# Sliding-window attention followed by a two-layer network on one core: most of the second layer by one level of Strassen's method

## The chip, the cores and the metric

The kernel runs on one core of one Trainium2 chip. The metric is device time in microseconds (us), from the start of the program to its end on that core; a time quoted here is the median of several executions unless it says otherwise. Lower is better. The five engines of the core appear as PE (TensorE, matrix products), DVE (VectorE), ACT (ScalarE), POOL (GpSimd) and SP (SyncE, which issues transfers). PEld is the loading of weights into PE, which runs beside its products.

## The reference

Attention over 4 batches of 768 tokens, 8 heads of 64, where a token sees the first 4 tokens and the last 128; then, on all 3072 tokens, a dense layer, a squared relu and a second dense layer.

```python
scores = scale * np.matmul(q, k.transpose(0, 1, 3, 2))
keep = is_sink | in_window                       # n_sink = 4, window = 128
scores = np.where(keep, scores, -1000000000.0)
a = np.exp(scores - np.max(scores, axis=-1, keepdims=True))
a = a / (np.sum(a, axis=-1, keepdims=True) + 1e-09)
attn_out = np.matmul(a, v)                       # (4, 8, 768, 64)
x = attn_out.transpose(0, 2, 1, 3).reshape(3072, 512)
r = np.maximum(x @ w_in, 0.0)                    # w_in 512 x 2048
return ((r * r) @ w_out).astype(np.float32)      # w_out 2048 x 512
```

The kernel holds its operands in bf16 and accumulates in fp32.

## The kernel before

The program doesn't write its instructions in the order of its text. It first lists operations, each with the engines that could do it, estimated durations, the operations that it must follow and the buffers that it takes. A planner then simulates the engines and emits the operations one by one in the order, and on the engine, that comes out earliest; `key` breaks ties between operations that could start at the same time.

```python
LATENCY = 0.2
PE_SLACK = 0.334
...
                for e, c in o.engines.items():
                    slack = PE_SLACK if e == "pe" else 0.0
                    start = max([t + slack if t > 0 else 0.0, engine.get(e, 0.0)] +
                                [a.end + LATENCY + slack for a in o.after if a.engine != e or a.dma] +
                                [a.issued for a in o.follow])
                    if pick is None or start + c < pick[1] + pick[2]:
                        pick = (e, start, c)
                cand = (round(pick[1], 2), o.key)
```

Attention computes the scores of a block of 256 tokens, takes exp on ACT, masks the result on DVE or POOL, multiplies with v, normalises into `xn_sb` and turns that into `xT` (by PE and a copy, or for batches 2 and 3 by a transposing DMA):

```python
                            if e == "dve":
                                mk = (mask if s else mask0).rearrange("p h a c -> p h (a c)")
                                nc.vector.tensor_mul(x[:, :, o:512], x[:, :, o:512], mk[:, :, o:512])
                            ...
                            else:
                                y = x.rearrange("p h (i g c) -> p g (h i) c", i=2, g=2)
                                for i in range(2):
                                    triangles(y[:, i], i, 4)         # an affine select on POOL
```

The two dense layers. `pm` and `py` are PSUM tiles of two banks each, and both come from one pool of two:

```python
    def layer1(b, key, fbs, c0, cw, need):
        ...
            for i, fb in enumerate(fbs):
                for kb in range(NKB):
                    nc.tensor.matmul(pm[:, i, :], lhsT=w_in_sb[:, fb // 4, kb, fb % 4:512:4],
                                     rhs=xT[:, c0 // 256:(c0 + cw) // 256, kb, :], start=(kb == 0), stop=(kb == NKB - 1))
        ...
                nc.scalar.activation(out=r, in_=bank_t.pop(tag), func=AF.Relu)
        ...
            (nc.vector if e == "dve" else nc.gpsimd).tensor_mul(
                gT_sb[c0 // 512][:, fbs[0]:fbs[0] + n, c0 % 512:c0 % 512 + cw], r, r)

    def layer2(b, u, keys, by_part=False):
        ...
                for fb in range(4 * part, 4 * part + 4):
                    nc.tensor.matmul(pm[:, i, :], lhsT=gT_sb[t // 4][:, fb, 128 * (t % 4):128 * (t % 4) + 128],
                                     rhs=w_out_sb[:, fb, :], start=(fb == 0), stop=(fb == NFB - 1))
```

Layer 2 takes a pair of token tiles (2 x 128 tokens) at a time: 32 products of 512 columns, then one copy out of PSUM and one store. There are 12 pairs, three a batch.

The softmax here doesn't subtract the row's maximum and nothing guards it: scores larger than these inputs give would overflow.

Of the kernel before, what the change touches and what calls it, by code (L numbers as in the profile page):

```python
# [16 lines left out]
LATENCY = 0.2  # L17
PE_SLACK = 0.334
DMA_START = {"sp": 1.2, "act": 1.2, "pool": 1.6}
DMA_LATENCY = 0.9  # L20
WARM_UNTIL = 34.0

# [10 lines left out]
class Op:  # L33
    def __init__(self, key, engines, run, after, takes, reads, dma, follow):
        self.key, self.engines, self.run = key, engines, run
        self.after, self.takes, self.reads, self.dma = list(after), list(takes), list(reads), dma
        self.follow, self.yields, self.margin = list(follow), [], 0.0
        self.end = self.issued = self.engine = None


class Plan:
# [8 lines left out]
    def __init__(self, capacity):  # L50
        self.ops, self.capacity = [], dict(capacity)

    def op(self, key, engines, run, after=(), takes=(), reads=(), dma=0.0, follow=()):
        o = Op(key, engines, run, after, takes, reads, dma, follow)
        self.ops.append(o)
        return o

    def run(self):
# [12 lines left out]
        while left:  # L71
            best = None
            for o in ready:
# [7 lines left out]
                for p, n in need.items():  # L81
                    if len(free[p]) < n:
                        ok = False
                        break
                    t = max(t, sorted(free[p])[n - 1] + LATENCY)
# [48 lines left out]
def kernel(  # L134
# [23 lines left out]
    NSINK = 4  # L158
# [4 lines left out]
    sizes = dict(att=2, den=2, qr=5, qs=6, expm=8, r=3, osb=2)  # L163
# [9 lines left out]
    mask = consts.tile([128, 2, 4, 128], BF16)  # L173
    mask0 = consts.tile([128, 2, 4, 128], BF16)
    bias = consts.tile([128, 4, 128], BF16)
    bias0 = consts.tile([128, 4, 128], BF16)
# [10 lines left out]
    xT_sb = [consts.tile([128, NS, NKB, 256], BF16, name=f"xT{i}") for i in range(2)]  # L187
    gT_sb = [consts.tile([128, NFB, w], BF16, name=f"gT{i}") for i, w in enumerate((512, 256))]
# [15 lines left out]
    def copy(e, dst, src):  # L204
        if e == "act":
            nc.scalar.activation(out=dst, in_=src, func=AF.Copy)  # L206
        elif e == "dve":
            nc.vector.tensor_copy(out=dst, in_=src)  # L208
        else:
            nc.gpsimd.tensor_copy(out=dst, in_=src)  # L210
# [41 lines left out]
    def build_masks(e):  # L252
        for h2 in range(2):
            for i in range(2):
                nc.gpsimd.tensor_copy(out=mask[:, h2, 2 * i:2 * i + 2, :], in_=tri)
                nc.gpsimd.tensor_copy(out=mask0[:, h2, 2 * i:2 * i + 2, :], in_=tri)
            nc.gpsimd.memset(mask0[0:NSINK, h2, 1:3, :], 1.0)
# [10 lines left out]
    c_fill = op(-9, {"dve": 2.5}, fill)  # L268
# [26 lines left out]

    def load_w_in(i, behind=None, yields=()):
# [24 lines left out]
    ROW = {256: 0.0205, 512: 0.028, 1024: 0.046, 1536: 0.068}  # L321
# [80 lines left out]
    def attention(b, key):  # L402
# [16 lines left out]
        def stage(g, f0, f1, side):  # L419

# [24 lines left out]
            for m in range(0, NP, w) if b not in NATURAL else ():  # L445
# [21 lines left out]
                def transpose(e, m=m, bs=bs):  # L467
                    pt = bank_t[b, m, g] = bank(bs, "pt", [128, 2, 1024], BF16)
                    warm(pt[:, 0, 0:128])
                    qs = {ti: qs_t.pop((b, m, ti, g)) for ti in (1, 0)}  # L470
                    for j in range(w):
                        for ti in (1, 0):
                            for t in range(n):

                                o = 128 * n * ti if w == 2 else 0
                                nc.tensor.matmul(  # L476
                                    pt[:, j if w == 2 else ti, o + 128 * t:o + 128 * t + 128],
                                    lhsT=qs[ti][:, j, t, :, :], rhs=ident, is_transpose=True,
                                    start=(t == 0 and (w == 1 or ti == 1)), stop=(t == n - 1 and (w == 1 or ti == 0)))
                tr = op(at(f + 0.03), {"pe": 0.02 + 0.11 * n * w}, transpose,  # L480
                        after=regs + [c_ident] + prev_scores + prev_sinks,
                        takes=[bs], reads=[qs_slot[b, m, ti, g] for ti in (0, 1)])
                ops["transpose", b, m, g] = tr
                for j in range(2):
                    def unload(e, m=m, j=j):

                        if w == 2:
                            copy(e,
                                 qkT_sb[:, m + j, :, t0 // 128:last // 128, :].rearrange(
                                     "c i a b -> c i (a b)").rearrange("c i (p t) -> c i p t", t=n),  # L490
                                 bank_t[b, m, g][:, j, 0:256 * n].rearrange("c (i t p) -> c i p t", i=2, t=n))
                        else:
                            copy(e,
                                 qkT_sb[:, m, j, t0 // 128:last // 128, :].rearrange(
                                     "c a b -> c (a b)").rearrange("c (p t) -> c p t", t=n),
                                 bank_t[b, m, g][:, j, 0:128 * n].rearrange("c (t p) -> c p t", t=n))
                    c = op(at(f + 0.04), {"dve": 0.1 + w * n * 0.14, "act": 0.19 + w * n * 0.107}, unload,
                           after=[tr] + prev_scores + prev_sinks, reads=[bs])
# [5 lines left out]
            if g == 0:  # L504
# [7 lines left out]
                def sink_values(e):  # L512
                    for j in range(NP):
# [9 lines left out]
                                    after=([ops["turn", b, 1, 0]] if b in NATURAL else copies) + prev_sinks)  # L523
            lo = max(256, t0)
# [20 lines left out]
            for s in range(t0 // 256, last // 256):  # L545
                fs = 0.36 + 0.5 * (256 * s - t0) / (last - t0)
                norms = []
                biased = b == 0 and s < BIASED
                for m0 in (0, 2):
# [27 lines left out]
                    for ms in ((m0,), (m0 + 1,)) if b == 0 else ((m0, m0 + 1),):  # L577
                        sc.append(op(
                            at(fm), {"pe": len(ms) * (0.7 if biased else 0.28) + 0.1}, lambda e, f=scores, ms=ms: f(e, ms),
                            takes=[banks[m - m0] for m in ms],  # L580
                            after=[ops["turn", b, ti, t] for ti in (0, 1)
# [5 lines left out]
                    for j, m in enumerate((m0, m0 + 1)):  # L587
# [7 lines left out]
                        def domask(e, s=s, m=m, o=o):  # L595
                            x = ex_t[b, s, m]
                            if e == "dve":
                                mk = (mask if s else mask0).rearrange("p h a c -> p h (a c)")
                                nc.vector.tensor_mul(x[:, :, o:512], x[:, :, o:512], mk[:, :, o:512])  # L599
                            elif s == 0:  # L600
                                mk = mask0.rearrange("p h a c -> p h (a c)")
                                nc.gpsimd.tensor_mul(x[:, :, o:512], x[:, :, o:512], mk[:, :, o:512])
# [4 lines left out]
                        if biased:  # L607
# [4 lines left out]
                                         {"pool": 1.3, "dve": 0.7} if s else {"dve": 0.58, "pool": 1.1},  # L612
                                         domask, after=[ex] if first else [ex, late["masks"]]))

                    bo = Slot(side, 1)

                    def values(e, s=s, m0=m0, bo=bo):
                        po = bank_t["o", b, s, m0] = bank(bo, "po", [128, 2, 512], FP32)
                        warm(po[:, 0, 0:128])
                        for j, m in enumerate((m0, m0 + 1)):  # L620
                            x = ex_t.pop((b, s, m))
                            pv = po[:, j, 0:4 * (D + 1)].rearrange("p (i h d) -> p i h d", i=2, d=D + 1)
                            mms = []
                            for h2 in range(2):
                                h = 2 * m + h2
                                for i in range(2):
                                    t = 2 * s + i
                                    if t >= 1:
# [247 lines left out]
```

## Time and profile before

| | before |
|---|---|
| median of 3 runs | 226.12 us (225.82 to 226.16) |
| span of the profiled run | 223.8 us |
| first product of layer 1 | 20.76 us |
| last product of layer 2 ends | 219.87 us |
| PE, DVE, ACT, POOL busy | 215.5, 103.7, 115.9, 64.8 us |

Two more lines of the kernel before are needed later. The first is one row of the table of stretches, from 53 to 78 us; its columns are the stretch, its length, the busy time of PE, PEld, DVE, ACT and POOL with the number of instructions, the clock, the share of the DMA engines and GB/s:

```profile
53.00:78.00 25.00, 24.41 (x274) 18.30 (x277) 16.58 (x31) 16.70 (x23) 21.38 (x25) 1.00 1.89 156
```

PE is idle for 25.00 - 24.41 = 0.59 us in it, and DVE is busy for two thirds. The second is from the groups of instructions by form, the masking on POOL:

```profile
L222 POOL TENSOR_SCALAR_AFFINE_SELECT expm<-expm 128x512 bf16<-128x512 bf16 x2 | 1.2, 634 | 6.5 <-ACT expm L590 6.5
```

Only two such selects are done here after the start, 634 ns each. The other masks are products on DVE.

### The profile page before, as it was taken

How to read it: one execution, taken by the hardware profiler on the slowest of the kernel's cores; microseconds unless marked ns; L12 is line 12 of the kernel's file. 1: busy time of each engine (PE TensorE's matmuls, PEld its weight loads, DVE VectorE, ACT ScalarE, POOL GpSimd, SP SyncE). 2: the span in 40 equal slices, each digit the busy share in tenths (PEclk: the TensorE clock that was granted, in tenths of full speed). 3: DMA queues.
4: the chain of work that ended last, by engine and by line, in shares of the span. 5: the costliest groups of instructions: out<-in, count | busy, mean ns of one | idle time of the engine just before them, and what ended most of it. 6: DMA issues, size and time to landing. Idle time of an engine off the chain costs nothing.

```text
span 223.8 us, 4586 instructions
## 1 busy us (share of the span) xinstructions
PE 215.5 (96%) x1932; PEld 138.2 (62%) x1952; DVE 103.7 (46%) x192; ACT 115.9 (52%) x131; POOL 64.8 (29%) x99
## 2 busy tenths in 40 slices
PE   7899999999999999999999999999999999999993
PEld 7549996467865886555454545598464455874441
DVE  6646346476656764466452536657241024430010
ACT  2695566506893577286727188665351165551010
POOL 7991015055999415997100000000000000000000
PEclk9999999999999999999999999999999999999999
DMA  5999968998999999999999464020221320000222
GB/s 144 289 187 208 208 196 109 199 349 240 131 179 139 150 197 150 122 150 199 143 144 124 139 166 48 0 50 0 47 98 25 116 97 0 0 3 0 94 103 86
DMA packets 84309, 28.13 MB, mean 126 GB/s; under 512 B 70336, under 2 KB 80832, under 8 KB 84288
## 3 DMA queue, kind: packets, MB, share of 16 engines
q0 software_dynamic: 52608, 10.49, 61.9%
q1 hardware_dynamic: 31496, 17.20, 34.9%
q8 instruction: 15, 0.25, 0.4%
q10 hardware_dynamic: 184, 0.14, 0.2%
q14 instruction: 6, 0.05, 0.1%
HBM read 27.30 MB, written 6.29 MB: 150 GB/s over the span
## 4 chain that ended last, share of the span: by engine, by line
PE 91%; DMA 3%; SPq 2%; ACT 1%; DVE 1%; issue 1%; DVEq 0%
PE pm L694 38%; PE py L734 37%; PE po L634 6%; PE ps L571 5%; DMA qr<-in_q_dram 3%; PE pt L476 2%; SPq L348 2%; PE px L671 1%; DVE qkT L208 1%; PE ps L564 1%; PE pk L531 0%; ACT r L703 0%; ACT expm L590 0%; ACT qkT L206 0%; PE px L201 0%
## 5 line engine op out<-in xcount | busy, mean ns | idle before, releaser
L734 PE MATMUL py<-w_out_sb,gT 128*128 128x512 bf16 x366 | 86.1, 379 | 1.1 <-issue 0.3
L694 PE MATMUL pm<-xT,w_in_sb 128*128 128x256 bf16 (+1 forms) x576 | 86.7, 308 | 0.4 <-ACT r L703 0.3
L694 PEld LDWEIGHTS <-w_in_sb 128*128 128x128 bf16 x576 | 63.0, 114 | 20.9 <-issue 1.7
L703 ACT ACTIVATE r<-pm 128x1024 bf16<-128x1024 f32 x48 | 49.2, 1025 | 32.7 <-PE pm L694 23.9
L734 PEld LDWEIGHTS <-gT 128*128 128x128 bf16 x384 | 35.4, 98 | 39.2 <-issue 1.7
L710 DVE TENSOR_TENSOR gT<-r 128x1024 bf16<-128x1024 bf16 x48 | 33.1, 690 | 50.3 <-ACT r L703 50.2
L590 ACT ACTIVATE expm<-ps 128x1024 bf16<-128x1024 f32 (+1 forms) x48 | 43.2, 952 | 17.1 <-PE ps L571 17.1
L599 DVE TENSOR_TENSOR expm<-expm,mask 128x1024 bf16<-128x1024 bf16 (+1 forms) x39 | 25.4, 654 | 23.7 <-ACT expm L590 23.2
L206 ACT ACTIVATE osb<-py 128x1024 f32<-128x1024 f32 x9 | 9.2, 1024 | 31.2 <-PE py L734 31.1
L634 PEld LDWEIGHTS <-expm 128*128 128x128 bf16 x352 | 16.5, 97 | 4.1 <-issue 0.6
L634 PE MATMUL po<-v,expm 128*128 128x65 bf16 x352 | 17.5, 193 | 0.0
L646 DVE TENSOR_TENSOR xn_sb<-po,rc 128x512 bf16<-128x512 f32 x24 | 16.6, 691 | 0.8
L571 PE MATMUL ps<-qkT 64*128 64x128 bf16 (+1 forms) x256 | 14.8, 238 | 0.3
L571 PEld LDWEIGHTS <-qkT 64*128 64x128 bf16 x256 | 8.0, 94 | 10.7 <-issue 9.9
L634 PE MATMUL po<-vs,es 128*128 128x65 bf16 x128 | 13.1, 193 | 0.0
L208 DVE COPY osb<-py 128x1024 f32<-128x1024 f32 (+2 forms) x4 | 3.6, 889 | 19.0 <-PE py L734 15.9
L210 POOL CAST qs<-qr 128x512 bf16<-128x512 f32 x6 | 4.2, 714 | 26.2 <-DVE gT L710 14.1
L634 PEld LDWEIGHTS <-es 128*128 128x128 bf16 x128 | 11.7, 97 | 0.0
L390 POOL DMA_DIRECT2D v<-in_v_dram x12 | 10.8, 918 | 3.4 <-DMA qn<-in_q_dram 2.5
L380 POOL DMA_DIRECT2D qn<-in_q_dram x12 | 10.8, 918 | 1.5 <-DMA qn<-in_k_dram 1.2
L361 POOL DMA_DIRECT2D v<-in_v_dram x12 | 10.9, 926 | 0.5 <-DMA qr<-in_k_dram 0.5
L208 DVE CAST qs<-qr 128x512 bf16<-128x512 f32 x16 | 8.1, 513 | 6.2 <-DMA qr<-in_k_dram 3.1
(51 smaller groups left out, 108.1 us busy)
## 6 DMA issues: line engine op xcount, KB each, us to landing
out_dram<-osb SPq DMA_DIRECT2D x11, 512.0 KB, 2.8
v<-in_v_dram POOLq DMA_DIRECT2D x24, 128.0 KB, 6.5
qr<-in_k_dram SPq DMA_DIRECT2D x8, 256.0 KB, 5.2
qr<-in_q_dram SPq DMA_DIRECT2D x8, 256.0 KB, 4.9
w_in_sb<-in_moe_w_in_dram POOLq DMA_DIRECT2D x4, 512.0 KB, 9.8
w_out_sb<-in_moe_w_out_dram POOLq DMA_DIRECT2D x4, 512.0 KB, 10.8
qn<-in_k_dram POOLq DMA_DIRECT2D x12, 128.0 KB, 7.2
qn<-in_q_dram POOLq DMA_DIRECT2D x12, 128.0 KB, 8.8
```

What stands on the lines that cost most here:

```text
L208: nc.vector.tensor_copy(out=dst, in_=src)
L361: return [nc.gpsimd.dma_start(out=v_sb[b % 2][:, t, :, 0:D], in_=v[b, :, 128 * t:128 * t + 128, :].rearrange("h p d -> p h d"))]
L380: return [nc.gpsimd.dma_start(out=qn_t[b, ti][:, t, :].rearrange("p (h d) -> p h d", d=D), in_=(q, k)[ti][b, :, 128 * t:128 * t + 128, :]. ...
L571: nc.tensor.matmul(ps[:, h2, o:o + w], lhsT=qkT_sb[r, m, 1, c, :], rhs=qkT_sb[r, m, 0, qb:qb + w // 128, :], start=(i == 0 and not biased) ...
L590: nc.scalar.activation(out=x[:, :, o:512], in_=bank_t["s", b, s, m][:, :, o:512], func=AF.Exp, scale=scale)
L599: nc.vector.tensor_mul(x[:, :, o:512], x[:, :, o:512], mk[:, :, o:512])
L634: nc.tensor.matmul(pv[:, i, h2, :], lhsT=lhsT, rhs=rhs, start=(n_ == 0), stop=(n_ == len(mms) - 1))
L646: nc.vector.tensor_tensor(out=xn_sb[:, 2 * s:2 * s + 2, 128 * m0:128 * m0 + 256].rearrange("p i (j h d) -> p j i h d", j=2, d=D), in0=pv[: ...
L694: nc.tensor.matmul(pm[:, i, :], lhsT=w_in_sb[:, fb // 4, kb, fb % 4:512:4], rhs=xT[:, c0 // 256:(c0 + cw) // 256, kb, :], start=(kb == 0), ...
L703: nc.scalar.activation(out=r, in_=bank_t.pop(tag), func=AF.Relu)
L710: (nc.vector if e == "dve" else nc.gpsimd).tensor_mul(gT_sb[c0 // 512][:, fbs[0]:fbs[0] + n, c0 % 512:c0 % 512 + cw], r, r)
L734: nc.tensor.matmul(pm[:, i, :], lhsT=gT_sb[t // 4][:, fb, 128 * (t % 4):128 * (t % 4) + 128], rhs=w_out_sb[:, fb, :], start=(fb == 0), sto ...
```

## The change

The intent has four parts.

- **Strassen.** For ten of the twelve pairs, the 256 x 2048 by 2048 x 512 product of layer 2 is cut into 2 x 2 blocks and done in seven block products instead of eight. Four sums of blocks of the activations a pair (`s1` to `s4`) and four sums of weight blocks, once, are new work for DVE, and so are the sums of the products.
- **Unordered banks.** A tile of two banks used to be one thing for the scheduler: a read of it waited for every earlier write. `touch` now declares that accesses to different banks of a tile, by PE and another engine, need no order.
- **A finer start.** For the first 512 tokens keys are transposed before queries arrive, values and norms go head pair by head pair, and the turn into `xT` goes in two halves.
- **A table of shifts** (`PLACES`) of the planner's keys, with smaller planned latencies. The masks become smaller constants, so that room is free, and a masking that the planner gives to DVE reads `tri`.

```diff
-LATENCY = 0.2
-PE_SLACK = 0.334
+LATENCY = 0.145
+PE_SLACK = 0.0
+PLACES = {
+    ('att', 0, 0): (-0.11, 0.89), ('att', 0, 1): (0.01, 0.98), ('att', 1, 0): (0.12, 1.07),
 ... (85 groups of operations in all)
+    def touch(t, e, ins, *banks, alone=False):
+        before = touched.setdefault(t, [])
+        for e_, ins_, banks_, alone_ in before:
+            apart = (e == "pe") != (e_ == "pe") or e != e_ and alone and alone_
+            if apart and not set(banks) & set(banks_):
+                tc.declare_no_dep(ins.ins, ins_.ins, reason="other bank")
+        before.append((e, ins, banks, alone))
 ...
 ... transposes: keys, then queries
+                for part in ((1,), (0,)) if w == 1 else ((1, 0),):
 ... values and norms by head pair
+                    parts = ((0,), (1,)) if b == 0 and s < 2 else ((0, 1),)
 ... relu: reads PSUM at a step of two, so that a tile gets the even tokens, the next the odd ones
+            h = bank_t.pop(tag).rearrange("p n (a q e) -> p (n a) e q", q=128, e=2)
+            o = r.rearrange("p n (a e q) -> p (n a) e q", q=128, e=2)
 ...
+        for n, x, y in ((1, b12, b11), (3, b22, b12), (2, b22, 1), (4, b21, 2)):
 ...
+                nc.vector.tensor_tensor(out=wt_sb[n], in0=x, in1=y, op=ALU.subtract)
 ... layer2_fast, for all pairs but the first two of batch 0
+        o1 = total("s1", a21, a22, ALU.add, s1_, key(0), low + high, [])
+        o3 = total("s3", a11, a21, ALU.subtract, None, key(0), low + [o1], [])
+        o2 = total("s2", "s1", a11, ALU.subtract, s2_, key(0), [o1], [s1_])
+        o4 = total("s4", a12, "s2", ALU.subtract, s4_, key(0), [o2], [s2_])
 ...
+        p5 = product(0, "c", "s1", 1, True, [o1, ops["wt", 1]], [bs], [s1_])
+        p7 = product(1, "d", "s3", 3, True, [o3, ops["wt", 3]])
+        x0 = taken("x", "c", os_, 0, [p5])
+        p1 = product(2, "a", a11, w(0, 0), False, low, [ys] if tail else [])
+        p6 = product(3, "b", "s2", 2, False, [o2, ops["wt", 2], x0], (), [s2_])
+        u0 = taken("u", "a", us, 2, [p1])
+        ex = pair_sum("x", "d", 2, [x0, p7 if tail else p1])
+        p3 = product(4, "c", "s4", w(1, 1), False, [x0, o4], (), [s4_])
+        p4 = product(5, "d", a22, 4, False, [ex, ops["wt", 4]] + ([] if tail else [u0]))
+        eu = pair_sum("u", "b", 4, [u0, p3])
 ...
+        p2 = product(6, "a", a12, w(1, 0), False, [u0] + high)
```

Each `product` is eight matmuls of 256 columns. `c` and `b` lie in the first bank of the pair's tile and `d` and `a` in the second, and `taken` and `pair_sum` read one bank while the next product fills the other.

## The prediction

> **What bounds the kernel now.** First the page's head: busy time of each engine.
>
> ```profile
> PE 215.5 (96%) x1932; PEld 138.2 (62%) x1952; DVE 103.7 (46%) x192; ACT 115.9 (52%) x131; POOL 64.8 (29%) x99
> ```
>
> TensorE (PE) is busy for 96% of a 223.8 us span (the timed median, 226.12 us, is 2.3 us more; I carry that difference over), VectorE (DVE) and ScalarE (ACT) for about half. A busy PE may still be a waiting PE, so next the chain that ended last, in order of time:
>
> ```profile
> 4.50 5.75 DMA qr<-in_q_dram
> ...
> 10.35 0.50 DVE qs L208
> 10.85 1.80 DVE qkT L208 x3
> ...
> 12.67 0.60 ACT qkT L206
> 13.27 0.92 ACT expm L590
> ...
> 18.03 0.45 PE po L201 x8
> 18.48 0.73 PE po L634 x24
> 19.20 0.45 PE px L671 x8
> 19.65 0.56 PE px L201 x10
> 20.21 0.53 PE px L671 x8
> ...
> 20.76 14.13 PE pm L694 x128
> ...
> 75.80 3.50 PE pm L694 x32
> ...
> 199.40 10.74 PE py L734 x49
> 210.14 0.05 issue
> 210.19 9.67 PE py L734 x44
> 219.87 0.02 issue
> 219.89 0.39 ACT half L206
> 220.28 0.02 issue
> 220.31 0.42 DVE osb L208
> ```
>
> Three stretches. To 20.76 us the chain passes from the last load of q through DVE and ACT to PE: latency of the first 512 tokens. L201 in it are warming matmuls, which compute nothing. From 20.76 to 219.87 us (199.1 us) every piece but about 1.1 us is PE work. After 219.87 us come two evictions, one behind the other although neither reads what the other writes, and the last store. So a matmul removed after 20.76 us should shorten the end by its issue time, if what replaces it on the other engines keeps up.
>
> The price of a matmul comes from the chain, not from the group's mean (379 ns for `py`, which overlaps its neighbours). From 199.13 to 219.87 us PE does three pairs of token tiles, 96 matmuls of 512 columns (94 are recorded): 20.74/96 = 0.216 us. Those of 256 columns cost 3.50/32 = 0.1094 us and 14.13/128 = 0.1104 us. Each has its own weight load, so a load per 256 columns is hidden in this kernel already.
>
> The durations that the new vector work needs are in the groups by form:
>
> ```profile
> L710 DVE TENSOR_TENSOR gT<-r 128x1024 bf16<-128x1024 bf16 x48 | 33.1, 690 | 50.3 <-ACT r L703 50.2
> L646 DVE TENSOR_TENSOR xn_sb<-po,rc 128x512 bf16<-128x512 f32 x24 | 16.6, 691 | 0.8
> ```
>
> The first is a bf16 two-operand instruction of 1024 elements (0.69 us), the second reads 512 fp32 elements of PSUM with a second operand (0.69 us).
>
> **What the Trainium skill says.** "TensorE: Matmul & The Clock Gate", section "Back-to-back issue gap", gives N/2.4 + 2.5 ns: 215.8 for 512 columns, 109.2 for 256. The trace agrees with both (216 and 109.4). The 131 ns that the same section gives for a stream with N = 512 isn't what this trace shows.
> "VectorE: DVE Perf Modes", section "The perf-mode tier table", has bf16 tensor_tensor at 2x, 1224 ns for 2048 elements, and its errata section an fp32 form of (N+151)/0.96 ns. With two elements a cycle 1024 bf16 give (512+151)/0.96 = 691 ns, and the trace has 690. I use these for sizes that the trace lacks.
> "PSUM — Partial Sum Buffer", section "PSUM bank collisions raise a hardware error", lets two engines be in different banks at the same time and not in one. The change declares only accesses to different banks independent; the two last evictions read one bank and stay in order.
> "SBUF — State Buffer", section "Door 1: The DMA port swizzle", says PSUM has 8-byte lines and that reads with less than two hits a line are slower. The new relu reads PSUM fp32 at a step of two, one hit a line. No instruction of the kernel before reads PSUM so, so the trace can't answer; it is a rival below.
>
> **The change part by part.** *Strassen.* Ten of the twelve pairs of token tiles (all but the first two of batch 0) become seven products of 128 x 1024 by 1024 x 256: 56 matmuls of 256 columns for 32 of 512. Before 32 x 0.216 = 6.91 us; after 56 x 0.1094 to 0.1104 = 6.13 to 6.18. Saved 0.73 to 0.78 a pair; ten pairs, 7.6 us, all on the path if PE stays fed.
>
> *Its price on the other engines, per pair.* Four sums of 1024 bf16: 4 x 0.69 = 2.76 us of DVE. Two sums of PSUM with an fp32 tile of 256: estimated (256+151)/0.96 = 0.42 each. One in SBUF of the same size, 0.42. One of 512 from PSUM, 0.69. Sum on DVE 4.7 us. Three copies of 256 columns, 0.38 on ACT (as the last eviction shows) or 0.42 on DVE, take the place of one copy of 1.02 us, so ACT is about even. Over ten pairs DVE gains 47 us, plus once 4 x 1.22 = 4.9 us for the weight sums: 103.7 to about 155 us, some 72% of a shorter span. Beside PE's 6.15 us a pair this still fits.
>
> Busy time by stretch shows where it fits badly:
>
> ```profile
> 53.00:103.00 50.00, 49.29 (x520) 34.21 (x525) 31.50 (x57) 33.20 (x41) 38.58 (x48) 1.00 2.07 156
> 103.00:150.00 47.00, 46.79 (x395) 26.44 (x398) 23.64 (x42) 27.72 (x31) 2.64 (x4) 1.00 0.97 112
> 150.00:199.10 49.10, 48.84 (x374) 30.50 (x375) 17.18 (x28) 22.16 (x23) 0.00 (x0) 1.00 0.14 44
> ```
>
> The columns after the length are PE, PEld, DVE, ACT, POOL. The first stretch has 31.5 us of DVE; 66 recorded matmuls of layer 2 lie in it, about two pairs, so 9.4 us of new work and perhaps the 4.9 us of weight sums: 46 of 50 us. That is close to full, though the plan can give relu or copies to ACT (33 us) and masks to GpSimd. The other two stretches rise to about 33 and 31 us, with ample slack. A product lasts 0.88 us and each eviction (0.4 us and a semaphore) has at least one other product to hide in, so in a pure layer-2 stretch nothing should wait. I put 0.9 us of new PE waits against the saving, nearly all before 103 us; this is a judgement and not a count.
>
> *First 512 tokens.* Keys are transposed before queries have come, values and norms go head pair by head pair, the turn of the result goes in two halves that ACT and DVE copy at the same time (0.6 us for 1.02, a gain of 0.4). From 10.25 to 20.76 us the trace has 22 warming matmuls; the chain charges 0.27 + 0.45 + 0.56 = 1.28 us to them. The plan puts them where it expects a gap, so smaller planned gaps mean fewer. Layer 1 of the first 256 tokens needs only those, yet starts after most of the work of the second 256. A full reordering could give more, but PE has its other work to do before or after anyway. I take 1.4 us, of which 0.4 from the copies and 1.0 from warming and order.
>
> *End.* The two last evictions handle 128 columns each instead of 256 (0.81 us with the issue pieces becomes about 0.55): 0.25 us. The last store keeps its latency. The rest of this tile pair leaves during the last product.
>
> *Masks, unordered banks, stores of 4 KB a partition.* The mask building on GpSimd shrinks; PE waited for none of it. Unordered banks are what lets the Strassen evictions run beside products; elsewhere PE hardly waits, so by themselves they are worth nothing after 20.76 us. Stores are not on the path.
>
> Sum: 226.1 - 7.6 - 1.4 - 0.25 + 0.9 = 217.7 us.
>
> **Rivals.** *DVE becomes the bound between 50 and 103 us.* For: 46 of 50 us by the count above, and every sum must precede its product. Against: ACT and GpSimd have room, PE has layer 1 and attention to do in between, and only that third is full. If DVE falls behind by 3 to 4 us, the time is 220 to 221.
>
> *The strided relu is slow.* For: the skill's line rule. If the 48 relus went from 1.02 to about 1.9 us, ACT would gain 42 us, to 158, and layer 1 would wait at its two buffers: PE spends 1.75 us on each 1024-column group, so such a relu no longer hides. The saving would be gone: 224 to 230 us. Against: ACT takes 1.02 us for 1024 elements, one at a time, so there may be nothing to lose, and the plan still budgets the old time. I give it one chance in twenty.
>
> *Buffers.* A Strassen pair holds a double bank through seven products and two evictions, and layer 1 alternates with it on the same two; one staging buffer of five is kept for a weight sum. If this ends in waits of some 0.2 us a pair, it costs 2 us: 219.
>
> *Better than thought.* Products of 256 columns free PE at a finer grain and the new order also closes what gaps there are: no new waits and 2.5 us at the start give 215.5.
>
> **Range and chances.** The matmul count is certain to some 0.3 us; the start is good for 0.5 to 2.5 and the new waits for 0 to 4. That gives 215.0 to 221.3 as the 8-in-10 range. Two per cent faster is 221.6; only a slow relu or a badly starved DVE miss it: faster 0.92, same 0.07, slower 0.01.
>
> **What would show it.** PE should have 240 more matmuls in layer 2 (560 + 64 instead of 384), at 0.109 to 0.110 us each in the chain's last stretch, about 18.4 us from its first product to its last. DVE busy should be near 155 us and relu still 1.02 us. Layer 1 should begin near 19.4 us. The stretch from there to the last matmul should be 191 to 193 us. A chain with pieces of DVE in the middle third, or gaps on PE put down to DVE sums, says that the first rival holds; gaps behind relu say the second. I am wrong outright if the 256-column products cost over 0.12 us each, or if waits for sums exceed 4 us.

## The result, and the profile after

| | before | after |
|---|---|---|
| median, runs of one chip | 226.14 us (225.82 to 226.56, 4 runs) | 220.86 us (220.63 to 221.37, 4 runs) |
| ratio | | 0.9765 (0.9746 to 0.9785): faster |
| span of the profiled run | 223.8 us | 219.2 us |

All ratios here are the mean time of one kernel's fast runs over that of the kernel before in the same rounds, so they are not quite the ratio of the medians. The result lies inside the predicted range, 3.2 us above the predicted time.

The page's head and, from the groups by form, relu and the selects on POOL:

```profile
PE 208.1 (95%) x2168; PEld 159.6 (73%) x2168; DVE 150.9 (69%) x291; ACT 116.1 (53%) x150; POOL 70.8 (32%) x98
```

```profile
L792 ACT ACTIVATE r<-pm 128x1024 bf16<-128x1024 f32 x48 | 49.3, 1026 | 43.3 <-PE pm L781 39.7
L273 POOL TENSOR_SCALAR_AFFINE_SELECT expm<-expm 128x512 bf16<-128x512 bf16 x12 | 10.3, 884 | 59.3 <-ACT expm L654 59.3
```

DVE has gone from 103.7 to 150.9 us, near the 155 of the prediction. Relu still takes 1026 ns. But twelve selects run on POOL instead of two, and each takes 884 ns instead of 634: something slows them.

The chain that ended last, in order of time (start, length, what):

```profile
10.70 9.77 DMA w_in_sb<-in_moe_w_in_dram
...
20.51 8.93 PE pm L781 x80
...
57.48 1.13 DVE wt L860
...
67.62 1.16 DVE sg L888
68.78 1.82 DVE expm L663 x2
...
70.64 0.36 PE po L704 x6
...
119.80 8.77 DMA xT<-xn_sb
...
128.62 1.89 PE pm L781 x8
...
196.73 13.97 PE py L927 x128
...
215.11 0.29 ACT half L247
...
215.42 0.29 DVE osb L249
```

Where the chain of the kernel before had only PE work, this one has 14 us of DVE (56.2 to 70.6 us, among them weight sums at L860, activation sums at L888 and masks at L663) and a transposing DMA at 119.8 us for which PE stood still. From 196.73 us PE does nothing but the last three pairs, 168 products of 256 columns, until 215.09 us, 0.02 us before the first of the two evictions: 18.36 us, or 0.1093 us each.

The same stretches as before, in the same columns:

```profile
53.00:78.00 25.00, 22.21 (x310) 18.27 (x308) 24.29 (x40) 18.97 (x29) 25.00 (x29) 1.00 2.10 171
103.00:150.00 47.00, 45.70 (x476) 33.50 (x475) 34.19 (x62) 27.82 (x34) 12.58 (x14) 1.00 1.01 109
```

From 53 to 78 us DVE is busy for 24.3 of 25 us (16.6 before) and PE is idle for 2.79 us (0.59). From 103 to 150 us PE is idle for 1.30 us (0.21), nearly all of it the wait for the DMA at 127 to 128.6 us.

**The account.** To compare the kernels although their order differs, I take the moment when PE has done 96 products of layer 1: in the kernel before 20.76 + 96 x 14.13/128 = 31.36 us, in the changed one 20.51 + 8.93 = 29.44 us (16 of the 96 ran at 17.97 us, ahead of the row shown).

| stretch | before | after | gain | predicted |
|---|---|---|---|---|
| start to 96 products of layer 1 | 31.36 | 29.44 | 1.92 | 1.4 |
| from there to the last product | 188.51 | 185.65 | 2.86 | 7.6 - 0.9 = 6.7 |
| last product to the end | 3.9 | 4.1 | -0.2 | 0.25 |
| span | 223.8 | 219.2 | 4.6 | 8.35 |

The three last pairs took 20.74 us before and 18.36 us after: 0.79 us saved a pair, 7.9 us for ten. Of these only 2.9 arrived, so the middle has 5.0 us of new delay on PE. The two stretches above hold 2.2 and 1.1 us of it as idle time. The rest is in the same waits. In an unbroken row products of 256 columns start 109 ns apart, but each is listed with 273 ns, because its end is modelled. So a listed end lies 0.16 us behind the moment at which the next product could start, and every wait looks 0.16 us shorter than it is. These are PE's waits of the changed kernel after its 96th product of layer 1 (who waited, for whom: us in total, times, longest):

```profile
PE pm L781 <- DMA xT<-xn_sb: 1.3, 1, 1.3
...
PE po L704 <- DVE expm L663: 0.5, 1, 0.5
PE py L927 <- DVE gT L888: 0.5, 1, 0.5
PE po L704 <- issue: 0.4, 1, 0.4
PE pt L533 <- DVE qkT L249: 0.4, 1, 0.4
PE pt L533 <- DVE qs L249: 0.3, 1, 0.3
PE ps L634 <- ACT r L792: 0.3, 1, 0.3
PE ps L634 <- ACT expm L654: 0.3, 1, 0.3
PE py L819 <- ACT r L792: 0.2, 1, 0.2
```

Nine waits, 4.3 us as listed, are 5.8 us when 0.16 us is added to each. The kernel before waits once there, for ACT, 0.3 us as listed and 0.5 us so corrected; the rest of its idle time is gaps of 0.05 to 0.16 us where records of products are missing. The difference, 5.3 us, covers the delay of 5.0 us.

The third row needs care. The sum that it names is `s3`, and the product is the pair's first, which reads `s1`; that one was done 0.8 us earlier. An exp on ACT ended 0.01 us before `s3`, and without any activation sums (below) the same wait is as long and is put down to that exp. So no wait in this list is shown to be a product's for its activation sum. The rows that end with ACT, and by this reading the third as well, are products that need nothing that relu or exp writes; by the kernel's text they share only PSUM tiles with them. These four waits are 1.4 us as listed, 2.0 us corrected.

### The profile page after: what moved, and what is told of

It is laid out like the page before. It is cut to its first block, busy times and chain, and to the rows that moved or that the text cites. A ratio compares the mean times of both kernels' runs of the same rounds, so it can differ in the third digit from the quotient of the medians.

```text
span 219.2 us, 5185 instructions
## 1 busy us (share of the span) xinstructions
PE 208.1 (95%) x2168; PEld 159.6 (73%) x2168; DVE 150.9 (69%) x291; ACT 116.1 (53%) x150; POOL 70.8 (32%) x98
## 4 chain that ended last, share of the span: by engine, by line
PE 75%; DMA 8%; DVE 7%; POOL 4%; issue 1%; SPq 1%; ACT 1%; POOLq 0%
PE pm L781 35%; PE py L927 22%; PE py L819 7%; PE po L704 5%; DMA w_in_sb<-in_moe_w_in_dram 4%; DMA xT<-xn_sb 4%; PE ps L634 3%; POOL v L413 2%; DVE wt L860 2%; DVE sg L888 1%; DVE expm L663 1%; PE pt L533 1%; DVE gT L799 1%; PE px L753 1%; PE ya L927 1%
## 5 line engine op out<-in xcount | busy, mean ns | idle before, releaser
L792 ACT ACTIVATE r<-pm 128x1024 bf16<-128x1024 f32 x48 | 49.3, 1026 | 43.3 <-PE pm L781 39.7
L654 ACT ACTIVATE expm<-ps 128x1024 bf16<-128x1024 f32 (+1 forms) x48 | 43.6, 955 | 10.5 <-PE ps L634 10.4
L927 PEld LDWEIGHTS <-gT 128*128 128x128 bf16 x320 | 30.8, 98 | 3.9 <-issue 0.2
L273 POOL TENSOR_SCALAR_AFFINE_SELECT expm<-expm 128x512 bf16<-128x512 bf16 x12 | 10.3, 884 | 59.3 <-ACT expm L654 59.3
L927 PEld LDWEIGHTS <-sg 128*128 128x128 bf16 x240 | 22.8, 98 | 4.9 <-issue 1.7
L927 PE MATMUL py<-wt,sg 128*128 128x256 bf16 x160 | 20.6, 273 | 0.5 <-DVE gT L888 0.5
L927 PE MATMUL py<-wt,gT 128*128 128x256 bf16 x160 | 20.7, 273 | 0.0
L927 PE MATMUL py<-w_out_sb,gT 128*128 128x256 bf16 x144 | 18.7, 273 | 0.0
L666 DVE TENSOR_TENSOR expm<-expm,tri 128x1024 bf16<-128x1024 bf16 x22 | 15.3, 707 | 4.5 <-ACT expm L654 4.4
L721 DVE TENSOR_TENSOR xn_sb<-po,rc 128x512 bf16<-128x512 f32 (+1 forms) x28 | 17.2, 615 | 1.0
L819 PE MATMUL py<-w_out_sb,gT 128*128 128x512 bf16 x64 | 15.8, 380 | 0.2 <-ACT r L792 0.2
L247 ACT ACTIVATE osb<-py 128x256 f32<-128x256 f32 (+1 forms) x14 | 6.3, 451 | 14.8 <-PE py L927 9.7
```

What stands on the lines that cost most here:

```text
L273: nc.gpsimd.affine_select(out=e_tile, in_=e_tile, compare_op=ALU.is_ge, fill=fill, base=i - 1, pattern=[[0, n], [1 if i else -1, 128]], ch ...
L654: nc.scalar.activation(out=x[:, :, o:512], in_=bank_t["s", b, s, m][:, :, o:512], func=AF.Exp, scale=scale)
L666: nc.vector.tensor_mul(y, y, tri.rearrange("p (o a) c -> p o (a c)", o=1).to_broadcast([128, 4, 256]))
L721: touch(("po", b, s, m0), e, nc.vector.tensor_tensor(out=xn_sb[:, 2 * s:2 * s + 2, 128 * (m0 + j0):128 * (m0 + j0 + nj)].rearrange("p i (j ...
L792: nc.scalar.activation(out=o, in_=h, func=AF.Relu)
L819: touch((b, u), e, nc.tensor.matmul(pm[:, i, :], lhsT=gT_sb[t // 4][:, fb, 128 * (t % 4):128 * (t % 4) + 128], rhs=w_out_sb[:, fb, :], sta ...
```

## The experiments

Twelve kernels ran, in rounds shared with the kernel before, all but one with three rounds and that one with five. The theory to test (A in the first expectations) says that DVE's work between 53 and 78 us delays PE; the rivals put the loss on the new order of PE's work, on the transposing DMAs, or on POOL's masks. Where a run is compared with the changed kernel, the medians come from different rounds, some on other chips; going by the ratios to the kernel before instead moves these differences by up to 0.4 us.

### No Strassen

```diff
-        if b == 0:
+        if False:
             weight_sums(0.6, ...)
 ...
+            if b > 0 or u == 2:
+                layer2(b, u, lambda i, part, u=u, b=b: b + 0.5 + 0.5 * (8 * u + 4 * i + part) / 24)
 ...
-    P.place(PLACES)
+    P.place({g: p for g, p in PLACES.items() if g[0] != "l2" or g in (("l2", 0, 0), ("l2", 0, 1))})
```

> The changed kernel with all twelve pairs by plain products, no sums, no weight sums. Theory A (Strassen saves 7.6 us of PE but VectorE overload between 53 and 78 us gives some 3.5 us back): PE has 7.6 us more to do and the waits of that stretch go, so about 224.5 us (220.9 + 7.6 - 4), and PE gaps there fall below 1 us. Rival B (the gaps of that stretch come from the order, GpSimd or buffers and not from the sums): about 228 us, gaps remain. Either way the distance to the kernel before is what the first 512 tokens and the end are worth, 1.5 to 2 us by my reading of the trace.

Measured: 228.60 us (228.52 to 228.72), ratio 1.0113 (1.0088 to 1.0139). In this order the rest of the change alone is no gain, and Strassen is worth 228.60 - 220.86 = 7.7 us on top of it. That this is close to the saving counted is partly chance, since both kernels wait: after its 96th product of layer 1 PE idles for 5.1 us here and for 4.3 us in the change. The number is the rival's. But the planner made a new order for this kernel, so the run doesn't say cleanly which: in its stretch from 53 to 78 us DVE is busy for only 15.9 us and PE is still idle for 1.77 us, which no load of DVE explains.

### Banks ordered again

```diff
     def touch(t, e, ins, *banks, alone=False):
-        before = touched.setdefault(t, [])
+        return
```

> The same instructions in the same order, but accesses of different banks of one tile are ordered again. If the unordered banks are what lets Strassen's evictions run beside the next product: each pair waits for about four evictions of 0.4 us and their semaphores, some 2.4 us a pair, 24 us over ten pairs less what the other work hides: 235 to 243 us. If they are only a refinement of the start: 221 to 222 us.

Measured: 233.22 us (232.50 to 234.85), ratio 1.0329. Same instructions, same order, 12.4 us slower than the change. The chain near the end of this run shows one pair:

```profile
205.16 1.92 PE py L927 x16
207.10 0.39 ACT u L247
207.52 0.43 DVE osb L948
208.00 1.92 PE py L927 x16
```

PE stands still while ACT and DVE read: 0.92 us, from 205.16 + 1.92 = 207.08 to 208.00. In the same way it stops for 0.46 us just before these rows and for 0.50 us just after them, 1.88 us in this pair. Ten such pairs would be 19 us, but not every pair stops so often: in the whole run PE waits 15 times for `taken` and `pair_sum`, 8.0 us as listed and 10.4 us with 0.16 us added to each, most of the measured loss. Without the unordered banks Strassen would lose against the kernel before.

### No weight sums (wrong result)

```diff
-                nc.vector.tensor_tensor(out=wt_sb[n], in0=x, in1=y, op=ALU.subtract)
+                wt_sb[n] = x
```

> Wrong result on purpose: the four weight sums are not computed (the products read quarters of w_out in their place), order of all other instructions unchanged; 5.2 us of VectorE less at 54 to 62 us. Theory A (VectorE is the bound between 53 and 78 us): 2 to 3.5 us faster, 217.4 to 218.9 us, and the PE gaps of 55 to 75 us mostly gone. Rival B (GpSimd, order or buffers): within 0.5 us of 220.9.

Measured: 219.58, 219.18 and 218.69 us in the fast runs (the profiled run, 224.16 us, was slow), ratio 0.9696. That is 1.7 us less than the change, below what A expects and far above what the rival does.

### The start in coarse steps

```diff
-                for part in ((1,), (0,)) if w == 1 else ((1, 0),):
+                for part in ((1, 0),):
-                    parts = ((0,), (1,)) if b == 0 and s < 2 else ((0, 1),)
+                    parts = ((0, 1),)
```

> Keys and queries transposed together, values and norms by two head pairs at once, as before; the halves of the turn stay. If the finer steps are what brings layer 1 forward (it begins at 18.0 us and not at 20.8): 1.2 to 2 us slower, 222 to 223 us, layer 1 from 19.5 us on. If the landing of the first layer's weights (20.5 us) sets the start anyway: within 0.5 us.

Measured: 225.16 us (223.86 to 227.17), ratio 0.997. At the start little is lost: the 96th product of layer 1 ends at 20.80 + 8.73 = 29.53 us, against 29.44. So the finer steps themselves are worth some 0.1 us by that mark, less than it varies: in four other runs with the order of the change it lies between 29.15 and 29.80 us. What brought the rest of the 1.9 us this run doesn't say. The other 4 us are lost later, in an order that the planner made anew. This run says nothing about where the change lost.

### No activation sums (wrong result)

```diff
-                nc.vector.tensor_tensor(
-                    out=t_[name], in0=x if not isinstance(x, str) else t_[x],
-                    in1=y if not isinstance(y, str) else t_[y], op=how)
+                t_[name] = {"s1": a21, "s2": a11, "s3": a21, "s4": a12}[name]
```

> Wrong result on purpose: the forty sums of activation blocks are not computed (products read the blocks themselves), order otherwise unchanged; 29 us of VectorE less, 2.9 us of it at 65 to 69 us. If PE waits for VectorE's load (theory A): 2 to 3 us faster, 218 to 219 us, and VectorE's masks near 69 us come on time. If the waits of that stretch come from the order of PE's own work, from ScalarE's row of exps or from GpSimd (theory B): within 0.8 us of 220.9, with gaps of 3 us or more left between 53 and 78 us.

Measured: 219.07 us (218.74 to 219.90), ratio 0.9704: 1.8 us less than the change, and the forty sums are gone. From 53 to 78 us PE is busy for 23.26 us and DVE for 21.40: PE's idle time falls from 2.79 to 1.74 us and no further, although DVE now has 3.6 us free:

```profile
53.00:78.00 25.00, 23.26 (x331) 19.41 (x329) 21.40 (x38) 19.27 (x30) 23.09 (x28) 1.00 2.14 151
```

Among the waits left is the one that the change's trace puts down to a sum, as long as before although there are no sums:

```profile
PE py L927 <- ACT expm L654: 0.5, 1, 0.5
```

### The last pair of batch 0 plain, with the weight sums early or late

```diff
-            if b == 0 and u < 2:
+            if b == 0:
                 layer2(b, u, ...)
```

and in the second kernel also `weight_sums(1.2, ...)` in place of `weight_sums(0.6, ...)`, which moves them behind batch 0.

> Batch 0's last pair by plain products, the other nine by Strassen; weight sums where they were. PE has 0.75 us more. If the late readiness of this one pair (weight sums, then squares, then four sums) is what starves PE between 53 and 78 us: 1 to 2.5 us faster, 218.4 to 219.9 us. If the stretch is starved for other reasons: 0.3 to 1 us slower.

> As the run with batch 0 plain, and the weight sums moved behind the full stretch, into one where VectorE has room. Theory A: another 0.5 to 1.5 us faster than that run, 217.5 to 219 us. Theory B: the same as that run within 0.5 us.

Measured: 230.12 us (229.13 to 231.30), ratio 1.0189, and in the fast runs of the second 227.70, 228.31 and 228.42 us, ratio 1.0100. Both miss by far what every theory expected. The waits of the first name the reason: PE's products stood for 5.0 us in three waits for activation sums on DVE, up to 2.5 us at once, where the change has no such wait over 0.6 us. In the new order the sums come too late for their products. These two runs answer nothing about batch 0, but they show how much a change of the list of operations does by the order alone.

### Masks given to DVE in the plan

```diff
-                                         {"pool": 1.3, "dve": 0.7} if s else {"dve": 0.58},
+                                         {"dve": 0.7} if s else {"dve": 0.58},
```

> No softmax mask on GpSimd: the twelve affine selects (0.63 to 1.08 us each) become six VectorE multiplies of 0.7. If GpSimd and VectorE hold each other up when both read SBUF (a mask on VectorE took 0.98 to 1.11 us beside the selects, and 0.55 or 0.69 alone): 0.5 to 1.5 us faster, 219.4 to 220.4 us, and no VectorE mask over 0.75 us. If VectorE's load is what counts: 0.5 to 1.5 us slower.

Measured: 224.01 us (222.44 to 225.23), ratio 0.9908: 3.2 us slower than the change. Again the order was made anew, and PE waits 2.8 us for sums that come late. So the next kernel keeps the order.

### Masks moved to DVE at the same place in the order

The planner still believes that these masks are POOL's, so every other instruction stays where it is. Only the emitted instruction differs:

```diff
-                            elif e == "dve":
+                            elif not (b == 0 and s < 2):
                                 y = x.rearrange("p h (i c) -> p (h i) c", i=2)
                                 nc.vector.tensor_mul(y, y, tri...)
```

> The order of every engine's program kept as in the changed kernel; the six masks that GpSimd did with two selects each are done by VectorE at the same place in the order, where the run with a new plan mixed this with new waits elsewhere. If GpSimd and VectorE hold each other up: 0.4 to 1.2 us faster than 220.9, no VectorE mask over 0.75 us, and no PE gap above 0.6 us at 69 to 73 us. If it is VectorE's load: 0 to 1 us slower.

Measured: 219.15 us (218.81 to 219.47), ratio 0.9698 (0.9676 to 0.9719), with a correct result. This beats both kernels. DVE does six more masks and is busy for less: 150.0 us against 150.9. The timelines show why. First the change, DVE and then POOL (start, length, engine, line, instruction):

```profile
67.62 1.16 DVE L888 TENSOR_TENSOR sg<-gT,sg 128x1024 bf16<-128x1024 bf16 x1
68.70 1.88 DVE L663 TENSOR_TENSOR expm<-expm,mask 128x768 bf16<-128x768 bf16 x2
```

```profile
68.39 3.73 POOL L273 TENSOR_SCALAR_AFFINE_SELECT expm<-expm 128x512 bf16<-128x512 bf16 x4
```

and the same place with the masks moved:

```profile
67.18 0.69 DVE L888 TENSOR_TENSOR sg<-gT,sg 128x1024 bf16<-128x1024 bf16 x1
67.79 0.55 DVE L663 TENSOR_TENSOR expm<-expm,mask 128x768 bf16<-128x768 bf16 x1
```

A sum that takes 0.69 us alone takes 1.16 us beside the selects, two masks of 0.55 us take 1.88, and the selects take 0.93 us each where they took 0.634 in the kernel before. (By the listed starts the first select begins 0.77 us after this sum, when alone it would have been done; spans on POOL are rough, so that these two meet is inferred.) The Trainium skill names it: "SBUF — State Buffer", section "Who interferes with whom", says that a VectorE instruction with two inputs in SBUF contends with a GpSimd instruction that reads SBUF. All these are of that kind, and the run without the selects agrees: no mask took more than 0.70 us. The six added masks are 6 x 0.685 = 4.1 us of work, and DVE's busy time still fell by 0.9, so by this sum some 5.0 us of DVE's 150.9 in the change was blocking and not work. Added up over the nine DVE instructions that overlap a select and are slow, it is 3.7 us.

The stretches of this run:

```profile
53.00:78.00 25.00, 23.26 (x327) 19.27 (x327) 24.03 (x44) 19.09 (x29) 21.25 (x25) 1.00 1.93 147
103.00:150.00 47.00, 47.00 (x508) 34.78 (x507) 35.03 (x66) 27.97 (x36) 2.46 (x3) 1.00 0.89 109
```

PE's idle time falls from 2.79 to 1.74 us in the first and from 1.30 to nothing in the second. The wait for the transposing DMA has gone with the selects, and so has the wait for a mask at 70.6 us. With 0.16 us added to each wait, PE waits some 2.7 us less in all: 1.5 us by the DMA, 0.7 us by the mask, and 0.8 us by the two waits for casts and copies (`qs`, `qkT`), of which one is left and short; two others grew by 0.2 us together. No wait after the start is put down to POOL in the change, so its slower masks held nothing up by themselves. From 114 to 130 us the DMA engines are less busy than in the change (1.07 against 1.87 in the units of the table), and the slowest of these transposes took 7.0 us instead of 10.1. That loads issued by a freer POOL leave the DMA engines earlier fits this, but I did not test that link by itself.

### No transposing DMA for batch 2 (wrong result)

```diff
-                            nc.sync.dma_start_transpose(...)
+                            b != 2 and nc.sync.dma_start_transpose(...)
```

> Wrong result on purpose: the six DMA transposes that turn batch 2's attention result are left out, all else in its order; layer 1 of that batch reads old data. If PE's wait of 1.5 us at 127 us is for the landing of these transposes alone: 1.0 to 1.6 us faster, 219.3 to 219.9 us, no gap there. If VectorE or the semaphores behind them would hold it as long: within 0.4 us.

Measured: 220.73 us (220.62 to 220.93), ratio 0.9769: no gain. PE no longer stops at 127 us, and the last product ends at 214.16 us instead of 215.09. But the stretch from there to the end of the span grew by 0.7 us, for which I have no cause. The same trace has the clearest picture of the blocking, first DVE and then POOL:

```profile
67.28 3.22 DVE L888 TENSOR_TENSOR sg<-gT,sg 128x1024 bf16<-128x1024 bf16 x1
```

```profile
67.56 2.39 POOL L273 TENSOR_SCALAR_AFFINE_SELECT expm<-expm 128x512 bf16<-128x512 bf16 x4
```

Here the selects run at full speed (0.60 us each), and one sum of 0.69 us waits for all four. Who gives way differs from run to run: in the change both were slowed.

### Without the table of shifts

```diff
-    P.place(PLACES)
+    P.place({})
```

> The changed kernel without the table of shifted keys: the same instructions, each placed where the planner's own keys put it. Three edits that changed only a few costs lost 3 to 9 us through new orders, so if the tuned order is worth as much as that suggests, this takes 224 to 232 us. If the order is worth little and those edits lost time by what they edited: 220.5 to 222.5 us.

Measured: 226.93 us (225.97 to 228.03), ratio 1.0043 (1.0005 to 1.0082). All the arithmetic of the change is in this kernel, and it gains nothing. The tuned order is worth 226.93 - 220.86 = 6.1 us.

A part of that comes by PE's clock, and not by waiting. The change's four runs had a mean granted clock of 0.995 to 1.000, these four 0.976 to 0.991, and the table of stretches shows a place (the clock is the third number from the end):

```profile
53.00:78.00 25.00, 20.85 (x248) 17.32 (x246) 21.95 (x38) 15.25 (x22) 18.74 (x22) 0.86 2.27 152
```

From 65.1 us the clock is half for 6.8 us, which costs at most some 25.00 x (1 - 0.86) = 3.5 us. The profiled runs of the other four kernels with a new order and Strassen, and the slow run without weight sums, also have stretches of 3.4 us at half clock. Of seven such places five lie at the end of a PE wait of 2.1 to 3.1 us; of the two others this is one, and one wait of 2.5 us had none. So a long wait may have cost twice, but no run tests that it is the cause. With the masks given to DVE, the one run at full clock took 222.44 us and the three at 0.992 took 223.76 to 225.23.

### Masks moved, and half of three weight sums earlier

Three half-size weight sums (rewritten so that they don't need the first one) run before 52 us, where DVE has room; the rest is the kernel with the masks moved.

```diff
+    def weight_half(n, h):
+        ...
+        x, y, how = {3: (b22, b12, ALU.subtract), 2: (wt_sb[3][:, top], b11, ALU.add),
+                     4: (b21, wt_sb[2][:, top], ALU.subtract)}[n]
+        nc.vector.tensor_tensor(out=wt_sb[n][:, top], in0=x, in1=y, op=how)
 ...
+                        if e == "dve" and b == 1 and "wt" not in late:
+                            for n_ in (3, 2, 4):
+                                weight_half(n_, 0)
```

> The version with all later masks on VectorE, and half of three of the four weight sums (2.1 us) moved, with no other change of order, from 54 to 62 us into the 2.5 us before 52 us in which VectorE waited. Leaving all weight sums out gained 1.5 us, so if VectorE's load between 53 and 78 us still holds PE: 0.3 to 0.9 us faster than the 219.15 us of the masks alone, 218.2 to 218.8 us. If what is left there is PE's own order (a row of score products that waits for ScalarE's exps): within 0.3 us of 219.15.

Measured with five rounds: 219.20 us (217.86 to 219.62), ratio 0.969 (0.9668 to 0.9711), correct, and not different from the masks moved alone. From 53 to 78 us DVE is busy for 23.02 us and PE for 23.34: against the kernel with the masks moved DVE is relieved by 1.0 us, and PE's idle time moves by 0.08 us.

```profile
53.00:78.00 25.00, 23.34 (x326) 19.27 (x324) 23.02 (x46) 19.16 (x29) 20.62 (x24) 1.00 1.99 145
```

**Taken together.** From 53 to 78 us PE is idle for 1.74 us with the masks moved (DVE 24.0 us), 1.66 with half the weight sums gone from there as well (23.0), and 1.74 without activation sums (21.4). So the change's 2.79 us have two parts. One, 1.05 us, goes when either the selects or the sums that they collide with go. The other doesn't shrink when DVE has less to do. With the masks moved, the waits that PE has left after its start are one of the values' for a normalising (0.5 us), one of 0.1 us for a cast, and four for exp and relu on ACT (1.5 us, with the one that the trace gives to a sum): single steps that come too close behind what they need, in the order that PE was given. The four look like waits for PSUM tiles; no run with more of them, or with another sharing, tests it.

## Why the prediction was right or wrong

**Saving per pair: right.** Products of 256 columns cost 0.1093 us with their own weight load, and a pair saved 0.79 us against 0.73 to 0.78 predicted. PE has 560 + 64 products in layer 2, as listed.

**Work on DVE: right in sum.** It is 150.9 us for about 155, and 4 to 5 us of that are blocking, so the work itself was over-counted by 8 to 9 us. Of these 3.5 us are five masks fewer on DVE (34 for 39), a relief that the prediction named and did not subtract.

**Relu at a step of two: right.** 1026 ns; the rival that rests on it is dead. The rival's "line rule" was in part the prediction's own: the page asks for two hits a line of SBUF, and where it gives PSUM's lines it speaks of matmuls alone.

**Unordered banks: right.** The prediction gave them no gain of their own and made them what lets evictions run beside products. Ordering them again costs 12.4 us.

**Start: right in direction, too small.** 1.9 us instead of 1.4. The reason was half right. The finer steps gave little (0.1 us by the mark of 96 products when they are undone), and the table of shifts no more than 0.4 (the mark is at 29.83 us without it), both within what the mark varies. There are fewer warming products, 48 recorded against 72, as the prediction expected; what they gave, and what the two halves of the turn gave, was not tested. Layer 1 began at 17.97 us and not at 19.4, but then waited for `w_in`, which landed at 20.47 us.

**End: wrong by some 0.4 us.** The two evictions became 0.29 us each, as said. But the stretch from the last product to the end grew from 3.9 to 4.1 us. The end now has four stores where there were three, and the last lands later; that the stores are the cause I only infer from this.

**New waits: this is the step that failed.** "I put 0.9 us of new PE waits against the saving, nearly all before 103 us; this is a judgement and not a count." The account gives 5.0 us (4.7 if the pairs saved only the 7.6 us that the prediction counted). The range allowed 0 to 4 us for it; that the total still lies inside, by 0.4 us, is owed to the start and the saving per pair, which gave 0.8 us more than the sum had. The place was right, the crowded third, and DVE's sums are in the chain there. But the size was off by a factor of five, and the mechanism was only near: no product is shown to wait for its sum. The sums stand in DVE's queue before casts, copies and masks of attention, and it is these that PE waited for. The runs show three parts of it:

- *The stretch was too long.* The prediction added the new work over 50 us and found 46 of 50. In the halves it is uneven: DVE went from 16.6 to 24.3 us between 53 and 78, while the next 25 us hold 18.3. An average over twice the length hid a full half.
- *The relief that it counted on was a cost.* It said that the plan could give "masks to GpSimd". The plan did, and these selects and DVE blocked each other. Moving them back to the busier engine gained 1.7 us in the medians (2.1 in the profiled runs), and took the stop at the transposing DMA away too.
- *Part of the loss isn't on DVE.* About 1.7 us of PE idle time between 53 and 78 us stayed in all three experiments that relieved DVE or took POOL out of its way; the kernel before had 0.59 there. Most of it is waits for exp and relu on ACT.

**The rivals.** "If DVE falls behind by 3 to 4 us, the time is 220 to 221" met the time, 220.86 us. Its cause is only partly right: taking out sums gains 1.7 to 1.8 us, but so does adding work to DVE when POOL is taken out of its way. These gains overlap and can't be added: with the masks moved, moving weight sums away as well gained nothing. Buffers as a rival were not tested by themselves, but the waits speak for a part of it: the four that end with ACT are 2.0 us, by the kernel's text for PSUM tiles, which is about the 2 us that the prediction gave this rival; the kernel before has 0.5 us of this kind.

**Two slips that change nothing.** "Every piece but about 1.1 us is PE work": the chain has 2.3 us of other pieces from 20.76 us on, 1.1 us about a relu and 1.2 us of issue, most of the latter where records are missing. And "better than thought" comes to 226.1 - 7.6 - 2.5 - 0.25 = 215.75 us and not 215.5.

What stays open: one wait of 0.4 us that the trace puts down to nothing, whether the waits for ACT would go with more PSUM tiles, the longer end of the run without transposes, and how much of the sums' gain is their load and how much the blocking that went with them.

## What to carry to other kernels

Check the load of a helping engine over stretches as short as the work that moves in (here 25 us, not 50), and count an engine that shares a path with it as no free helper: here it gained 1.7 us to move masks from the idler engine to the busier one. Where a planner makes the order, the order is part of the kernel: five edits that let it plan anew were 3 to 9 us slower than the change, in part at a lower clock, and four of them hid what they were to show, so an experiment should alter the emitted instruction and leave the plan alone. And arithmetic saved on the bounding engine is only gained if evictions run beside it; without the unordered banks the same Strassen was 7 us slower than the kernel before.

## What the Trainium skill lacked or had wrong

- "TensorE: Matmul & The Clock Gate", section "Back-to-back issue gap": its 131 ns for a stream of weight load and matmul with N = 512 isn't seen. Such streams here took 216 ns at 512 columns and 109.3 ns at 256, which is what its formula for the single gap gives.
- "SBUF — State Buffer", section "Door 1: The DMA port swizzle", asks for two hits a line of SBUF and says of PSUM, with its lines of 8 bytes, only that access that isn't contiguous slows matmuls; it has nothing on ScalarE's reads. Relu on ScalarE reading fp32 at a step of two took 1026 ns for 1024 columns, and about 1.02 us without the step: no cost for this instruction.
- "SBUF — State Buffer", section "Who interferes with whom", says that the two-input VectorE instruction contends with GpSimd's reads and that issue order decides who blocks, but gives no size for this pair. Measured: one sum of 0.69 us took 3.22 us, until four selects at full speed (0.60 us each) were done, although by the listed starts it began 0.28 us before them; in another run both slowed, the selects to 0.93 us each and the masks from 0.55 to 0.98.
